# A pair of attention heads as one unit in a routed-attention and mixer kernel

## The chip, the cores and the metric

One core of a Trainium2 chip runs the whole program. Its engines work side by side and meet through semaphores: TensorE (PE, matmuls; PEld, its weight loads), VectorE (DVE), ScalarE (ACT), GpSimd (POOL) and SyncE (SP), whose queue issues most DMA transfers. The metric is the device time of one execution in microseconds (us), the median of several runs. A profile gives one execution, instruction by instruction.

## The reference

The program is routed attention followed by an MLP mixer, on 4 batches, 8 heads, 768 positions, head size 64, 16 clusters.

```python
q_assign = argmax(q_n @ c_n.T)            # nearest of 16 centroids, normalised
k_assign = argmax(k_n @ c_n.T)
mask = q_assign[:, :, :, None] == k_assign[:, :, None, :]
scores = where(mask, q @ k.T / 8, -1e9)
attn = exp(scores - max); attn = attn / (attn.sum + 1e-9)
x = (attn @ v), heads side by side         # (4, 768, 512)

h  = relu(x.T @ w_tok1) @ w_tok2           # over positions, 256 wide
u  = x + h.T
out = u + relu(u @ w_ch1) @ w_ch2          # over channels, 1536 wide
```

All inputs and outputs are float32.

## The kernel before

Two heads are taken together, so there are 16 pairs (`NPAIR`). Heads lie on partitions 0 to 63 and 64 to 127. The 768 queries are worked in two halves (`qh`) of 384; the 768 keys are six chunks (`j`) of 128.

The mask costs no vector work: one-hot cluster vectors (`ohT`, bf16, a query's multiplied by a huge negative number) are multiplied on TensorE into the same PSUM tile as q and k, so that scores of other clusters are pushed far below and their exponential is 0.

```python
def scores(g, qh):
    for j in range(NJ):                               # six chunks of keys
        sc = ps_sc.tile([P, 2, 512], F32, tag="sc")   # 3 buffers in PSUM
        for src, start in ((st["ohT"], True), (st["T"], False)):
            for h in range(2):                        # 64-row tiles of the array
                nc.tensor.matmul(sc[:, h, 0:HS], lhsT=src[rows, 1, j], rhs=src[rows, 0, js], ...)
        ex = st["ex", j] = work.tile([P, 2, HS], F32) # 6 buffers
        nc.scalar.activation(out=ex, in_=sc[:, :, 0:HS], func=ACT.Exp, scale=SM_SCALE)

def add_up(g, qh):        # VectorE: five additions of 128 x 768, for the denominators
def values(g, qh):        # TensorE: av (64-column tiles) += va^T ex, six chunks; ScalarE copies av to avT
```

Small products on TensorE belong to each pair, with VectorE work behind them:

```python
def pair_sums(g, den)         # ones^T sum: denominators, 32-column tiles
def pair_denominators(g)      # VectorE 32x32 transposes of den
def pair_reciprocals(g)       # VectorE
def route_products(g, pr)     # centroids times turned q and k, 32-column tiles
def route(g)                  # VectorE: transpose, maximum, one-hots (oh)
def route_big(g)              # VectorE: the query's one-hots times the large number
def route_turn(g)             # SP: dma_start_transpose oh -> ohT
def route_count(g)            # ScalarE: counts for a guard at the end
def half_turn(g, qh, px)      # TensorE: three 128x128 transposes of avT
def half_out(g, qh)           # VectorE: px times reciprocals -> x
def turn(g)                   # VectorE: 32x32 transposes, turned q and k (st["T"])
def load(g)                   # SP: eight loads of q and k (128-byte rows), one of v
```

The MLP weights are loaded and rounded beside attention, in 21 steps (`rounding(n)` does the next n). Step i does the last part of piece i-2, the ScalarE part of piece i-1 and issues the load of piece i:

```python
def step(i=i):
    if 2 <= i: rest(...)                     # VectorE: wh, wh, wT (one buffer); GpSimd: wT + wup -> weight
    if 1 <= i <= len(pieces): scalar_part()  # ScalarE: wh and wup from raw
    if i < len(pieces): load_bits()          # SP: raw (3 buffers) from memory, 384 or 512 KB
```

The loop:

```python
for g in range(NPAIR):
    more, old, final = g < NPAIR - 1, g - 1, g == NPAIR - 1
    if g + 2 < NPAIR: load(g + 2)
    scores(g, 0)
    if g == 0: turn(1)
    add_up(g, 0); rounding(1); values(g, 0)
    two = ps_sc.tile([P, 2, 512], F32, tag="sc", name="small")
    pair_sums(old, two[:, 0, 0:HS]);  route_products(g + 1, two[:, 1, 0:HS])
    pair_denominators(old)
    route(g + 1); route_big(g + 1); route_turn(g + 1)
    pair_reciprocals(old)
    scores(g, 1)
    route_count(g + 1)
    add_up(g, 1); turn(g + 2); values(g, 1)
    two = ps_sc.tile([P, 2, 512], F32, tag="sc", name="px")
    half_turn(old, 0, ...); half_turn(old, 1, ...); half_out(old, 0); half_out(old, 1)
    rounding(g < EARLY or final)             # EARLY = 6
# ... conditions for the first and last pairs cut
```

Ahead of the loop a start-up part loads pair 0, routes it by TensorE transposes, and keeps TensorE warm with dummy matmuls. Behind it come the mixer's matmuls (`ph`, `pu`, then blocked products `pX`, `pY`, `pZ`), which the change does not touch.

Of the kernel before, what the change touches and what calls it, by code (L numbers as in the profile page):

```python
# [17 lines left out]
C = 16  # L18
P = 128
# [11 lines left out]
QP = P // NQ  # L31
NPAIR = B * NF

EARLY = 6
SM_SCALE = 0.125


# [8 lines left out]
def kernel(  # L46
# [37 lines left out]
            tc.tile_pool(name=name, bufs=bufs, reuse_waits="tile", **kw)  # L84
        )

    ps_w = pool("ps_w", 1, space=PSUM)
    ps_av = pool("ps_av", 1, space=PSUM)
    ps_sc_stack = fast.enter_context(ExitStack())
    ps_sc = pool("ps_sc", 3, ps_sc_stack, space=PSUM)  # L90

# [4 lines left out]
    staging = fast.enter_context(ExitStack())  # L96
    stage = pool("stage", 2, staging)
    attention = fast.enter_context(ExitStack())
    loads = pool("loads", 3, attention)
    small = pool("small", 2, attention)  # L100
    qktp = pool("qktp", 2, attention)
    work = pool("work", 6, attention)
    sums = pool("sums", 2, attention)

    routing = fast.enter_context(ExitStack())
# [24 lines left out]
    def load(g):  # L130


        b, f = divmod(g, NF)
        st = state.setdefault(g, {})
        st["qk"] = qkpool.tile([P, 2, NJ, NQ, QP], F32, name="qk")
        st["va"] = loads.tile([P, 2, NJ, D], F32, name="va")
        for a, src in ((1, k), (0, q)):
            for c in range(NQ):
                h, d0 = 2 * f + c // 2, (c % 2) * QP
                nc.sync.dma_start(  # L140
                    st["qk"][c * QP : (c + 1) * QP, a].rearrange("r j i d -> r (j i) d"),
                    src[b, h, :, d0 : d0 + QP].rearrange("(i r j) d -> r j i d", i=NQ, j=NJ),
                )
        nc.sync.dma_start(
            st["va"], v[b, 2 * f : 2 * f + 2].rearrange("h (p j) d -> p h j d", p=P)
        )
# [91 lines left out]
    def centroids_norm(cen):  # L238
        sq = rsmall.tile([P, D], F32, name="censq")
        ss = rsmall.tile([P, 1], F32, name="ss")  # L240
        nc.vector.tensor_tensor(out=sq, in0=cen, in1=cen, op=ALU.mult)
        nc.vector.reduce_sum(out=ss, in_=sq, axis=AX.X)
        lo = rsmall.tile([P, 1], F32, name="lo")
        nc.vector.tensor_scalar_max(out=lo, in0=ss, scalar1=float(2.0**-100))


        nrm = rsmall.tile([P, 1], F32, name="nrm0")
        nc.vector.tensor_scalar(
            out=nrm.bitcast(I32), in0=lo.bitcast(I32), scalar1=0.5, scalar2=float(0x1FBB6875),
            op0=ALU.mult, op1=ALU.add,  # L250
        )
        for it in range(2):
            rr = rsmall.tile([P, 1], F32, name="rr")
            nc.vector.reciprocal(out=rr, in_=nrm)
            tw = rsmall.tile([P, 1], F32, name="tw")
            nc.vector.scalar_tensor_tensor(
                out=tw, in0=ss, scalar=rr, in1=nrm, op0=ALU.mult, op1=ALU.add
            )
            nrm = rsmall.tile([P, 1], F32, name="nrm")
            nc.vector.tensor_scalar(  # L260
                out=nrm, in0=tw, scalar1=(0.5, 0.49984956)[1 - it], scalar2=(0.0, 1e-6)[it],
                op0=ALU.mult, op1=ALU.add,
            )
        rden = rsmall.tile([P, 1], F32, name="rden")
        nc.vector.reciprocal(out=rden, in_=nrm)
        cn = rsmall.tile([P, 2, D], F32, name="cn")
        nc.vector.tensor_scalar_mul(
            out=cn, in0=cen.unsqueeze(1).to_broadcast([P, 2, D]), scalar1=rden
        )
        pc = ps_w.tile([P, H * C], F32, tag="w", name="pc")  # L270
        nc.tensor.transpose(out=pc, in_=cn.rearrange("p i d -> p (i d)"), identity=ident)
        return pc

# [72 lines left out]


    def load_first():
        st = state[0] = {"qk": qkpool.tile([P, 2, NJ, NQ, QP], F32, name="qk")}
        st["va"] = loads.tile([P, 2, NJ, D], F32, name="va")  # L350
        st["T"] = qktp.tile([P, 2, NJ, P], F32, name="qkT")
        st["ohT"] = qktp.tile([P, 2, NJ, P], BF16, name="ohT")
        st["rows"] = st.pop("qk").rearrange("p a j i d -> p (a j i d)").rearrange(
            "p (n a j h d) -> p n a j h d", n=2, a=2, h=2, j=HJ
        )
        for n in range(2):
            for a, src, queue in ((1, k, nc.sync), (0, q, nc.scalar)):
                for h in range(2):
                    queue.dma_start(
                        st["rows"][:, n, a, :, h],  # L360
                        src[0, h].rearrange("(p j) d -> p j d", p=P)[:, HJ * n : HJ * n + HJ],
                    )
        nc.sync.dma_start(st["va"], v[0, 0:2].rearrange("h (p j) d -> p h j d", p=P))

    def turn_first(n, tiles):

        st = state[0]
        js = slice(HJ * n, HJ * n + HJ)
        for a in (1, 0):
            for j in range(HJ):  # L370
                nc.tensor.transpose(
                    out=tiles[a][:, j * P : (j + 1) * P],
                    in_=st["rows"][:, n, a, j].rearrange("p h d -> p (h d)"), identity=ident,
                )
        return [(st["T"][:, a, js].rearrange("p j t -> p (j t)"), tiles[a]) for a in range(2)]

    def route_turn_first(n):
        po = ps_w.tile([P, 2, HJ, P], BF16, tag="w", name="po")
        for a in (1, 0):
            for j in range(HJ):  # L380
                nc.tensor.transpose(
                    out=po[:, a, j], in_=ohs[0][:, a, HJ * n + j], identity=identb
                )
        return po
# [21 lines left out]
    def scores(g, qh):  # L406
        st = state[g]
        js = slice(HJ * qh, HJ * qh + HJ)
        for j in range(NJ):
# [3 lines left out]
            for src, start in ((st["ohT"], True), (st["T"], False)):  # L413
                for h in range(2):
# [2 lines left out]
                        sc[:, h, 0:HS], lhsT=src[rows, 1, j], rhs=src[rows, 0, js],  # L417
                        start=start, stop=not start,
                    )
            ex = st["ex", j] = work.tile([P, 2, HS], F32, name="ex")  # L420
            nc.scalar.activation(out=ex, in_=sc[:, :, 0:HS], func=ACT.Exp, scale=SM_SCALE)  # L421

    def add_up(g, qh):
        st = state[g]
        if qh == 0:
            st["sum"] = sums.tile([P, 2, 2, HS], F32, name="sum")
        acc = st["sum"][:, qh]
        for j in range(1, NJ):
            nc.vector.tensor_tensor(  # L429
                out=acc, in0=acc if j > 1 else st["ex", 0], in1=st["ex", j], op=ALU.add  # L430
            )

    def values(g, qh):
        st = state[g]
        av = ps_av.tile([P, HS], F32, name="av")
        for j in range(NJ):
            ex = st.pop(("ex", j))
            for h in range(2):
                nc.tensor.matmul(  # L439
                    av[h * D : (h + 1) * D], lhsT=st["va"][:, h, j], rhs=ex[:, h],  # L440
# [285 lines left out]
            nc.vector.tensor_reduce(out=good[:, i : i + 1], in_=ok, axis=AX.X, op=ALU.min)  # L726

    def fits_count():
        pn = ps_w.tile([1, 3], F32, tag="w", name="pn")
        nc.tensor.matmul(pn, lhsT=ones[:, 0:1], rhs=good, start=True, stop=True)  # L730
        nc.vector.tensor_copy(out=count, in_=pn)

# [8 lines left out]
    def begin():  # L741
# [11 lines left out]
        for oh in ohs:  # L753
            nc.gpsimd.memset(oh, 0.0)
        load(1)
        pw = ps_av.tile([P, HS], F32, name="av")

        def keep_warm(n):
            for _ in range(n):
# [29 lines left out]
    for b in range(B):  # L789
        if b + 1 < B:  # L790
            ends += [lambda b=b, t=t: tok1(b + 1, t) for t in range(NT)]
        ends += [lambda b=b, j=j: tok2(b, j) for j in range(NJ)]

    def rounding(n):
        for _ in range(min(n, len(weights))):
            weights.pop(0)()

    for g in range(NPAIR):
        more, old, final = g < NPAIR - 1, g - 1, g == NPAIR - 1
        if g + 2 < NPAIR:  # L800
            load(g + 2)
        if final:
            assert not weights
            routing.close()
            W["ch2"] = pool("wc2pool", 1, side="right").tile([P, NCT, DM], F32, name="wc2")
            weights = list(weight_steps(stage, W, ("ch2",)))

        scores(g, 0)
        if g == 0:
            turn(1)  # L810
        add_up(g, 0)
        rounding(1)
        values(g, 0)
        if more or old >= 0:
            two = ps_sc.tile([P, 2, 512], F32, tag="sc", name="small")
            if old >= 0:
                pair_sums(old, two[:, 0, 0:HS])
            if more:
                route_products(g + 1, two[:, 1, 0:HS])
            if old >= 0:  # L820
                pair_denominators(old)
            if more:
                route(g + 1)
                route_big(g + 1)
                route_turn(g + 1)
            if old >= 0:
                pair_reciprocals(old)

        scores(g, 1)
        if more:  # L830
            route_count(g + 1)
        add_up(g, 1)
        if g + 2 < NPAIR:
            turn(g + 2)
        values(g, 1)
        if old >= 0:
            two = ps_sc.tile([P, 2, 512], F32, tag="sc", name="px")
            for qh in range(2):
                half_turn(old, qh, two[:, qh, 0:HS])
            for qh in range(2):  # L840
                half_out(old, qh)
        rounding(g < EARLY or final)

    pair_sums(NPAIR - 1, ps_w.tile([P, HS], F32, tag="w", name="den"))
    pair_denominators(NPAIR - 1)
    pair_reciprocals(NPAIR - 1)
    ps_sc_stack.close()
    pools["ps_m"] = pool("ps_m", 2, space=PSUM)
    for m in range(9):
        ends.pop(0)()  # L850
        if m == 0:
            half_turn(NPAIR - 1, 0, ps_w.tile([P, HS], F32, tag="w", name="px"))
            half_turn(NPAIR - 1, 1, ps_av.tile([P, HS], F32, name="av"))
            for qh in range(2):
                half_out(NPAIR - 1, qh)
        if m % 3 == 2:
# [243 lines left out]
```

## Time and profile before

| | |
|---|---|
| time, median of 3 runs | 877.95 us (877.77 to 878.12) |
| span of the profiled execution | 875.5 us |
| start of the first scores | 10.14 us |
| start of the first mixer matmul (`ph`) | 333.06 us |
| one exponential, 128x768, on ScalarE | 811 ns |
| one addition, 128x768, on VectorE | 958 ns median |
| turning q and k of a pair, VectorE | 2 x 953 ns |

An engine's line in the busy table is the time in which it had an instruction running, its share of the span, and the number of instructions. In the slices each digit is a fortieth of the span, in tenths busy. The chain of waits is read back from the last instruction; each of its rows is a start, a length, an engine, a name and line, and how many instructions were merged. In a timeline a row reads: start, length, engine, line, operation, output<-inputs, shapes, count, and in brackets the idle time before it with what ended it. A matmul's row length holds its way through the array, so neighbouring matmuls overlap, and their cost is read from the distance between starts. A DMA row's last number is the median from issue to landing.

### The profile page before, as it was taken

How to read it: one execution, taken by the hardware profiler on the slowest of the kernel's cores; microseconds unless marked ns; L12 is line 12 of the kernel's file. 1: busy time of each engine (PE TensorE's matmuls, PEld its weight loads, DVE VectorE, ACT ScalarE, POOL GpSimd, SP SyncE). 2: the span in 40 equal slices, each digit the busy share in tenths (PEclk: the TensorE clock that was granted, in tenths of full speed). 3: DMA queues.
4: the chain of work that ended last, by engine and by line, in shares of the span. 5: the costliest groups of instructions: out<-in, count | busy, mean ns of one | idle time of the engine just before them, and what ended most of it. 6: DMA issues, size and time to landing. Idle time of an engine off the chain costs nothing.

```text
span 875.5 us, 11022 instructions
## 1 busy us (share of the span) xinstructions
PE 862.4 (99%) x4294; PEld 522.8 (60%) x4294; DVE 504.9 (58%) x848; ACT 297.8 (34%) x506; POOL 44.2 (5%) x40
## 2 busy tenths in 40 slices
PE   9999999999999999999999999999999999999996
PEld 4444444444444444444578686685876867768675
DVE  6798898888878862895553433423344333443332
ACT  4666566666556551321210211203112031130210
POOL 1010011000010000330000000000000000000000
PEclk9999999999999999999999999999999999999999
DMA  8665675544443130420000010000010000100001
GB/s 153 156 123 119 140 139 115 126 109 97 97 97 73 20 90 0 144 72 1 0 1 1 0 37 37 0 1 0 36 38 1 0 1 25 48 1 1 0 25 51
DMA packets 133275, 47.61 MB, mean 54 GB/s; under 512 B 122080, under 2 KB 126176, under 8 KB 133216
## 3 DMA queue, kind: packets, MB, share of 16 engines
q1 hardware_dynamic: 131616, 46.45, 23.0%
q8 instruction: 35, 0.57, 0.3%
q10 hardware_dynamic: 1600, 0.39, 0.2%
q14 instruction: 24, 0.20, 0.1%
HBM read 34.64 MB, written 6.29 MB: 47 GB/s over the span
## 4 chain that ended last, share of the span: by engine, by line
PE 95%; DVE 3%; ACT 1%; issue 0%; DVEq 0%
PE sc L416 18%; PE av L439 15%; PE pX L690 14%; PE pX L639 14%; PE pZ L690 7%; PE pZ L639 7%; PE ph L508 4%; PE pY L690 4%; PE pY L639 4%; PE pu L517 3%; PE px L468 1%; PE small L455 1%; PE pt L580 1%; PE small L296 1%; DVE wh L209 1%; DVE wT L214 1%
## 5 line engine op out<-in xcount | busy, mean ns | idle before, releaser
L421 ACT ACTIVATE ex<-sc 128x768 f32<-128x768 f32 x192 | 152.6, 811 | 44.8 <-PE sc L416 42.6
L416 PE MATMUL sc<-qkT 64*128 64x384 f32 x768 | 155.1, 482 | 0.0
L429 DVE TENSOR_TENSOR sum<-sum,ex 128x768 f32<-128x768 f32 x128 | 125.3, 979 | 13.7 <-ACT ex L421 0.5
L439 PE MATMUL av<-ex,va 128*64 128x384 f32 x768 | 130.9, 490 | 0.0
L439 PEld LDWEIGHTS av<-ex,va 128*64 128x64 f32 x768 | 52.2, 137 | 74.8 <-issue 71.0
L416 PEld LDWEIGHTS sc<-qkT 64*128 64x128 f32 x768 | 68.2, 188 | 34.8 <-issue 34.6
L639 PE MATMUL pX<-uT,wc 128*128 128x384 f32 x192 | 67.4, 487 | 0.0
L416 PE MATMUL sc<-ohT 64*128 64x384 bf16 x384 | 63.0, 324 | 0.3 <-DVE ohT L389 0.2
L647 ACT COPY p<-pX 128x384 f32<-128x384 f32 x24 | 11.4, 475 | 148.1 <-PE pX L639 148.1
L639 PEld LDWEIGHTS pX<-uT,wc 128*128 128x128 f32 x192 | 36.2, 190 | 24.7 <-issue 1.0
L221 POOL TENSOR_TENSOR wc<-wT,wup 128x512 int32<-128x512 int32 x24 | 32.0, 1334 | 253.5 <-ACT avT L446 132.0
L429 DVE TENSOR_TENSOR sum<-ex 128x768 f32<-128x768 f32 x32 | 32.0, 1001 | 20.3 <-ACT ex L421 20.2
L446 ACT COPY avT<-av 128x384 f32<-128x384 f32 x32 | 15.3, 479 | 83.1 <-PE av L439 83.1
L508 PE MATMUL ph<-x,wt 128*128 128x512 f32 x96 | 42.0, 594 | 1.2 <-DVE x L520 0.7
L517 PE MATMUL pu<-h,wt 128*128 128x512 f32 x96 | 42.0, 592 | 0.0
L534 DVE TENSOR_TENSOR c<-pZ,u 128x384 f32<-128x384 f32 x24 | 13.4, 557 | 46.9 <-PE pZ L639 46.9
L416 PEld LDWEIGHTS <-ohT 64*128 64x128 bf16 x384 | 19.2, 94 | 35.4 <-issue 13.6
L534 DVE TENSOR_TENSOR x<-pX,x 128x256 f32<-128x256 f32 x24 | 10.2, 423 | 49.3 <-PE pX L690 49.3
L534 DVE TENSOR_TENSOR hA<-pY,p 128x384 f32<-128x384 f32 x24 | 13.4, 557 | 40.4 <-PE pY L639 40.4
L690 PE MATMUL pX<-w2s,hA 128*128 128x256 f32 x144 | 35.1, 380 | 0.5 <-DVE x L534 0.5
L690 PE MATMUL pX<-wc,hA 128*128 128x256 f32 x144 | 35.0, 379 | 0.0
L690 PE MATMUL pZ<-w2s,hS 128*128 128x256 f32 x144 | 35.0, 379 | 0.0
(129 smaller groups left out, 1196.5 us busy)
## 6 DMA issues: line engine op xcount, KB each, us to landing
raw<-in_moe_w_ch_dram SPq DMA_DIRECT2D x24, 512.0 KB, 4.3
qk<-in_k_dram SPq DMA_DIRECT2D x64, 96.0 KB, 4.0
va<-in_v_dram SPq DMA_DIRECT2D x16, 384.0 KB, 4.0
out_dram<-x SPq DMA_DIRECT2D x24, 256.0 KB, 2.0
qk<-in_q_dram SPq DMA_DIRECT2D x60, 96.0 KB, 3.4
raw<-in_moe_w_tok_dram SPq DMA_DIRECT2D x3, 512.0 KB, 4.6
raw<-in_moe_w_tok_dram SPq DMA_DIRECT2D x4, 384.0 KB, 4.0
qk<-in_q_dram ACTq DMA_DIRECT2D x4, 96.0 KB, 3.1
```

Of the source, the lines that this page charges most:

```text
L221: nc.gpsimd.tensor_tensor(out=dst.bitcast(I32), in0=T, in1=up, op=ALU.add)
L416: nc.tensor.matmul(sc[:, h, 0:HS], lhsT=src[rows, 1, j], rhs=src[rows, 0, js], start=start, stop=not start,)
L421: nc.scalar.activation(out=ex, in_=sc[:, :, 0:HS], func=ACT.Exp, scale=SM_SCALE)
L429: nc.vector.tensor_tensor(out=acc, in0=acc if j > 1 else st["ex", 0], in1=st["ex", j], op=ALU.add)
L439: nc.tensor.matmul(av[h * D : (h + 1) * D], lhsT=st["va"][:, h, j], rhs=ex[:, h], start=(j == 0), stop=(j == NJ - 1),)
L446: nc.scalar.copy(out=st["avT"][:, js].rearrange("p j t -> p (j t)"), in_=av)
L508: nc.tensor.matmul(pf, lhsT=W["tok1"][:, j, t * P : (t + 1) * P], rhs=xs[b][:, j], start=(j == 0), stop=(j == NJ - 1),)
L517: nc.tensor.matmul(pu, lhsT=W["tok2"][:, t, j], rhs=h1s[b][:, t], start=(t == 0), stop=(t == NT - 1))
L534: nc.vector.tensor_tensor(out=dst, in0=a, in1=b, op=ALU.add)
L639: nc.tensor.matmul(psum, lhsT=A[a][:, k, c * P : (c + 1) * P], rhs=R[r][:, k], start=start and k == 0, stop=k == 1, skip_group_check=not s ...
L647: nc.scalar.copy(out=kept[name], in_=psum)
L690: nc.tensor.matmul(psum, lhsT=h2[a][:, k, i * P : (i + 1) * P], rhs=Bw[w][:, 3 * part + k], start=start and k == 0, stop=k == 2, skip_grou ...
```

## The change

A pair becomes one unit. All twelve chunks of scores (both query halves) run in one go, then all twelve of values, and then the pair's small products at one place: the transposes of the pair before, the sums of this pair, and the routing products of the pair after next. It is meant to let TensorE change between kinds of products less often. For that the exponentials get nine buffers instead of six (three more chunks can stand in PSUM), `av` gets two PSUM buffers (it takes over the bank of `ps_w`), v is loaded apart from q and k with two buffers instead of three, and routing runs two pairs ahead instead of one. The weight steps, of which there are still 21, are done at one place: two in even pairs below 12, else one.

```diff
-EARLY = 6
+EARLY = 12
+EX = 9
...
-    ps_w = pool("ps_w", 1, space=PSUM)
-    ps_av = pool("ps_av", 1, space=PSUM)
+    ps_av = pool("ps_av", 2, space=PSUM)
...
-    loads = pool("loads", 3, attention)
+    loads = pool("loads", 2, attention)
...
-    work = pool("work", 6, attention)
+    work = pool("work", EX, attention)
...
+    def route_on(g):
+        route(g)
+        route_big(g)
+        route_turn(g)
...
+    load_v(1)
     for g in range(NPAIR):
-        [the loop above]
+        final = g == NPAIR - 1
...
+        for qh in range(2):
+            scores(g, qh)
+            if g == 0 and qh == 0:
+                turn(1)
+                load(2)
+            add_up(g, qh)
         if g == 0:
+            route_products(1, ps_av.tile([P, HS], F32, tag="av", name="pr"))
+            route_on(1)
+        for other in (1, 2) if g == 1 else (g + 1,) if 2 <= g < NPAIR - 1 else ():
+            route_count(other)
         if g + 2 < NPAIR:
             turn(g + 2)
+        if g + 3 < NPAIR:
+            load(g + 3)
+        rounding(2 if final or g % 2 == 0 and g < EARLY else 1)
+        for qh in range(2):
+            values(g, qh)
+        if g + 2 < NPAIR:
+            load_v(g + 2)
+
+        if g > 0:
             two = ps_sc.tile([P, 2, 512], F32, tag="sc", name="px")
             for qh in range(2):
+                half_turn(g - 1, qh, two[:, qh, 0:HS])
+        two = ps_sc.tile([P, 2, 512], F32, tag="sc", name="small")
+        pair_sums(g, two[:, 0, 0:HS])
+        if g + 2 < NPAIR:
+            route_products(g + 2, two[:, 1, 0:HS])
+        if g > 0:
             for qh in range(2):
+                half_out(g - 1, qh)
+        pair_denominators(g)
+        if g + 2 < NPAIR:
+            route_on(g + 2)
+        pair_reciprocals(g)
```

Cut: in the start-up part the first rows of q and k are held in two of the nine exponential buffers instead of a q-and-k buffer, and the products that used `ps_w` use a buffer of `av`.

More of the change, by code (lines that the diff above doesn't have):

```diff
@@ L135, in load @@
         st["qk"] = qkpool.tile([P, 2, NJ, NQ, QP], F32, name="qk")
-        st["va"] = loads.tile([P, 2, NJ, D], F32, name="va")
         for a, src in ((1, k), (0, q)):
@@ L143, in load, with load_v @@
                 )
+    def load_v(g):
+        b, f = divmod(g, NF)
+        st = state[g]
+        st["va"] = loads.tile([P, 2, NJ, D], F32, name="va")
         nc.sync.dma_start(
@@ L269, in centroids_norm @@
         )
-        pc = ps_w.tile([P, H * C], F32, tag="w", name="pc")
+        pc = ps_av.tile([P, H * C], F32, tag="av", name="pc")
         nc.tensor.transpose(out=pc, in_=cn.rearrange("p i d -> p (i d)"), identity=ident)
@@ L348, in load_first @@
     def load_first():
-        st = state[0] = {"qk": qkpool.tile([P, 2, NJ, NQ, QP], F32, name="qk")}
-        st["va"] = loads.tile([P, 2, NJ, D], F32, name="va")
+        st = state[0] = {}
         st["T"] = qktp.tile([P, 2, NJ, P], F32, name="qkT")
         st["ohT"] = qktp.tile([P, 2, NJ, P], BF16, name="ohT")
-        st["rows"] = st.pop("qk").rearrange("p a j i d -> p (a j i d)").rearrange(
-            "p (n a j h d) -> p n a j h d", n=2, a=2, h=2, j=HJ
-        )
+        st["rows"] = [
+            work.tile([P, 2, HS], F32, name="ex").rearrange("p a (j h d) -> p a j h d", h=2, d=D)
+            for _ in range(2)
+        ]
         for n in range(2):
@@ L359, in load_first @@
                     queue.dma_start(
-                        st["rows"][:, n, a, :, h],
+                        st["rows"][n][:, a, :, h],
                         src[0, h].rearrange("(p j) d -> p j d", p=P)[:, HJ * n : HJ * n + HJ],
                     )
-        nc.sync.dma_start(st["va"], v[0, 0:2].rearrange("h (p j) d -> p h j d", p=P))
     def turn_first(n, tiles):
@@ L372, in turn_first @@
                     out=tiles[a][:, j * P : (j + 1) * P],
-                    in_=st["rows"][:, n, a, j].rearrange("p h d -> p (h d)"), identity=ident,
+                    in_=st["rows"][n][:, a, j].rearrange("p h d -> p (h d)"), identity=ident,
                 )
@@ L377, in route_turn_first @@
     def route_turn_first(n):
-        po = ps_w.tile([P, 2, HJ, P], BF16, tag="w", name="po")
+        po = ps_av.tile([P, 2, HJ, P], BF16, tag="av", name="po")
         for a in (1, 0):
@@ L419, in scores @@
                     )
-            ex = st["ex", j] = work.tile([P, 2, HS], F32, name="ex")
+            ex = st["ex", qh, j] = work.tile([P, 2, HS], F32, name="ex")
             nc.scalar.activation(out=ex, in_=sc[:, :, 0:HS], func=ACT.Exp, scale=SM_SCALE)
@@ L425, in add_up @@
         if qh == 0:
-            st["sum"] = sums.tile([P, 2, 2, HS], F32, name="sum")
+            st["sum"] = sums.tile([P, 2, 2, HS], F32, name="sum", bufs=1)
         acc = st["sum"][:, qh]
@@ L429, in add_up @@
             nc.vector.tensor_tensor(
-                out=acc, in0=acc if j > 1 else st["ex", 0], in1=st["ex", j], op=ALU.add
+                out=acc, in0=acc if j > 1 else st["ex", qh, 0], in1=st["ex", qh, j], op=ALU.add
             )
@@ L434, in values @@
         st = state[g]
-        av = ps_av.tile([P, HS], F32, name="av")
+        av = ps_av.tile([P, HS], F32, tag="av", name="av")
         for j in range(NJ):
-            ex = st.pop(("ex", j))
+            ex = st.pop(("ex", qh, j))
             for h in range(2):
@@ L728, in fits_count @@
     def fits_count():
-        pn = ps_w.tile([1, 3], F32, tag="w", name="pn")
+        pn = ps_av.tile([1, 3], F32, tag="av", name="pn")
         nc.tensor.matmul(pn, lhsT=ones[:, 0:1], rhs=good, start=True, stop=True)
@@ L755, in begin @@
         load(1)
-        pw = ps_av.tile([P, HS], F32, name="av")
+        load_v(0)
+        pw = ps_av.tile([P, HS], F32, tag="av", name="av")
         def keep_warm(n):
@@ L796, in rounding @@
             weights.pop(0)()
+    load_v(1)
     for g in range(NPAIR):
-        more, old, final = g < NPAIR - 1, g - 1, g == NPAIR - 1
-        if g + 2 < NPAIR:
-            load(g + 2)
+        final = g == NPAIR - 1
         if final:
@@ L806 @@
             weights = list(weight_steps(stage, W, ("ch2",)))
-        scores(g, 0)
-        if g == 0:
[L810 to L832, printed above, removed]
+        for qh in range(2):
[4 more added lines that the diff above has]
+            add_up(g, qh)
+        if g == 0:
+            route_products(1, ps_av.tile([P, HS], F32, tag="av", name="pr"))
+            route_on(1)
+        for other in (1, 2) if g == 1 else (g + 1,) if 2 <= g < NPAIR - 1 else ():
+            route_count(other)
@@ L833 @@
         if g + 2 < NPAIR:
             turn(g + 2)
-        values(g, 1)
-        if old >= 0:
+        if g + 3 < NPAIR:
[6 more added lines that the diff above has]
+        if g > 0:
             two = ps_sc.tile([P, 2, 512], F32, tag="sc", name="px")
             for qh in range(2):
-                half_turn(old, qh, two[:, qh, 0:HS])
-            for qh in range(2):
-                half_out(old, qh)
@@ L842 @@
[L842 to L846, printed above, removed]
+                half_turn(g - 1, qh, two[:, qh, 0:HS])
[4 more added lines that the diff above has]
+        if g > 0:
+            for qh in range(2):
+                half_out(g - 1, qh)
@@ L851 @@
         if m == 0:
-            half_turn(NPAIR - 1, 0, ps_w.tile([P, HS], F32, tag="w", name="px"))
-            half_turn(NPAIR - 1, 1, ps_av.tile([P, HS], F32, name="av"))
+            half_turn(NPAIR - 1, 0, ps_av.tile([P, HS], F32, tag="av", name="px"))
+            half_turn(NPAIR - 1, 1, ps_av.tile([P, HS], F32, tag="av", name="av"))
             for qh in range(2):
```

## The prediction

> **What bounds the kernel now.** I read the busy table first, then the slices, then the chain that ended last, then the timelines of single engines and of the DMA queue.
>
> ```profile
> PE 862.4 (99%) x4294; PEld 522.8 (60%) x4294; DVE 504.9 (58%) x848; ACT 297.8 (34%) x506; POOL 44.2 (5%) x40
> PE   9999999999999999999999999999999999999996
> ```
>
> TensorE (PE) is busy in every slice, so only two things count: what shortens its own stream, and what makes it wait. The attention loop is the first 333 us (the first `ph` matmul starts at 333.06). One steady pair of heads in the chain of waits (start us, us):
>
> ```profile
> 231.60 4.95 PE sc L416 x36
> 236.55 4.02 PE av L439 x24
> 240.57 0.78 PE small L455 x8
> 241.35 0.65 PE small L296 x8
> 242.00 4.95 PE sc L416 x36
> 246.95 4.02 PE av L439 x24
> 250.97 0.81 PE px L468 x6
> ```
>
> The next pair would begin at 251.78: 20.18 us, and TensorE waits for nobody in it. Now the pieces. Within a run of scores the timeline of TensorE shows one chunk every 0.8075 us:
>
> ```profile
> 232.35 0.33 PE L416 MATMUL sc<-ohT 64*128 64x384 bf16 x2
> ...
> 235.58 0.33 PE L416 MATMUL sc<-ohT 64*128 64x384 bf16 x2
> ```
>
> (235.58 - 232.35) / 4 = 0.8075. Six chunks are 4.845, the row has 4.95: 0.105 is lost at the turn from scores to values. The weight loads of values come every 0.322 us for two matmuls (from 227.07 to 229.97 in nine steps), so 24 matmuls are 3.87 and the row has 4.02: 0.15 is lost at the turn from values to the next kind.
>
> The other view that matters is the DMA queue, SP, in the first pairs, with the landing times of the page (last number, us):
>
> ```profile
> 22.78 1.58 SPq L341 DMA_TRANSPOSE ohT<-oh  x1
> 24.41 0.84 SPq L191 DMA_DIRECT2D raw<-in_moe_w_tok_dram  x1
> 25.30 3.45 SPq L140 DMA_DIRECT2D qk<-in_k_dram  x4
> 28.79 3.42 SPq L140 DMA_DIRECT2D qk<-in_q_dram  x4
> ```
>
> ```profile
> raw<-in_moe_w_tok_dram SPq DMA_DIRECT2D x3, 512.0 KB, 4.6
> ohT<-oh SPq DMA_TRANSPOSE x15, 3.8
> ```
>
> SP issues in program order. It sat from 20.6 until 22.78 for VectorE's one-hots, and all transfers behind the transposing one started after it. The eight loads of q and k take 5.8 to 6.9 us just to issue.
>
> **What the Trainium skill says.** *TensorEngine Tiling (Array Packing)*, Key Properties: changing the tiling mode drains TensorE. The trace agrees in kind: scores are 64*128 tiles, values 128*64, sums and routing 128*32, transposes 128*128, and each turn costs 0.1 to 0.15 us. *TensorE: Matmul & The Clock Gate*, Part 1, "Architectural detail": the queues of ScalarE and VectorE are strictly first in, first out; nothing in the trace overtakes. Same page, "What's actually happening": after an idle window of about 3.4 us TensorE falls to half clock and needs about as long of full work to come back. The trace has the cold start: twelve warm-up matmuls of 384 columns take 4.02 us, 0.335 each, where a bf16 matmul of 384 columns later costs 0.16 (0.8075 less 0.645 of float32 passes). The clock column shows 1.00 all the same, so I go by the durations. *Trainium Kernel Development and Optimization*, Key Constraints: the queues share 16 DMA engines, so it is the sequencer's issue order that I look at.
>
> **The change, part by part.**
>
> *Removed: turns.* Before, a pair has six: scores-values twice, values-small, small-scores, values-px, px-scores. After: scores-values, values-px, px-small, small-scores. A pair is 12 x 0.8075 + 0.105 = 9.795, 48 x 0.161 + 0.15 = 7.89, px 0.81 (the same 0.81 lies before a 128*32 product at 330.97 to 331.78), small 0.78 + 0.65 = 1.43. Sum 19.92, against 20.18: 0.26 less. For 16 pairs -4.1 us. The number of chunks, exponentials and additions does not change.
>
> *Added: exponentials 9 to 11 wait.* Nine buffers for twelve chunks: nine are written out, three scores stand in PSUM until values has read the first buffers. ScalarE starts 1.03 after the scores (242.96 against 241.93) and needs 0.807 each; number 9 can start when values has done one chunk, at 9.795 + 0.65 + 0.4 (tail of the last matmul) = 10.85. Number 11 ends at 13.3, and values wants it at 9.8 + 11 x 0.645 = 16.9. No wait. VectorE adds until 14.8 (1.03 each), turns the next q and k (1.83) until 16.6, rounds one weight piece (0.42 + 0.43 + 0.69, with gaps 1.6) until 18.2; px is ready at 18.6. No wait either.
>
> *Moved: two rounding steps at one place.* In even pairs below 12, VectorE rounds two pieces in a row, and `wT` has one buffer, read by GpSimd for 1.27 to 1.33 us. The second piece ends at about 20.3. The two `half_out` (1.02) and the two 32x32 transposes (0.58, 0.54) come after it, and chunks 1 and 2 of the next pair want their PSUM buffers at 20.7 and 21.5; they come free at about 21.4 and 22.4. That is some 0.9 us in pairs 2, 6, 8, 10 (in pair 4 the pieces are smaller, in pair 0 nothing is rounded yet): +3.5.
>
> *Moved: the first pair.* Here I expect the largest term. Routing of pair 1 now stands after all of pair 0's additions. Scores start at 10.14 as before; twelve chunks with `po` between them end at 20.4, the routing product at 21.2, values follow. Exponential 9 starts at 22.1, 11 ends at 24.5, the additions end at 26.0, the routing on VectorE takes 2.15 (20.57 to 22.72 before): 28.15. The transposing DMA lands 3.8 later, 32.0. TensorE, done with values at 29.1 and with both small products at 30.9 (it waits for the turned q and k until 30.0), starts pair 1 at about 32.0: 1 us lost.
>
> Worse is what SP holds behind that transfer. The build's order on SP is: transpose (waits for VectorE), eight loads for pair 3, then the first two weight pieces. So the first `raw` is issued at 28.2 + 1.5 + 6.0 = 35.7 and lands at 40.3. On ScalarE its `wh` and `wup` stand ahead of both `avT` copies and of all exponentials of pair 1: 40.3 + 1.3 + 0.9 = 42.4, first exponential until 43.2. Scores has three PSUM buffers and stops after three chunks, at 34.5. It stands still 8.8 us. An idle TensorE of that length should come back cold: half of about 4 us lost, +2. In later pairs the piece lands at 14 to 15 us after the scores' start, before the place where ScalarE wants it, so it happens once.
>
> Sum: -4.1 (turns) + 3.5 (double rounding) + 1.0 (late one-hots) + 8.8 (stall) + 2.0 (clock) = +11.2, so 889; I write 888, as the 3.5 is more likely too large than too small. The dense stage after the loop has the same instructions and no change.
>
> **The rivals.**
>
> 1. *Only the turns count: 874 (-4.1).* For it: TensorE is the bound in the whole trace, and buffers are counted to fit (nine and three make twelve). Against it: the first pair's queue order, which no buffer mends. This holds only if the first raw piece lands before about 33 us, and I see no way for it to.
> 2. *The stall but no double-rounding loss and no cold clock: 884.* VectorE has 58% of the span, though about 85% in the loop; a half microsecond of slack in the even pairs would do. This is near my lower end.
> 3. *Exponentials or additions become the bound in every pair: 893 or more.* VectorE's work in a pair is about 17 to 18.5 us of 19.92. If the additions run slower while GpSimd rounds (one addition took 1841 ns against a median of 958), each pair could lose 0.3 us, +5.
> 4. *A faster loop than the turns explain.* Nothing supports more: every product remains.
>
> **Range and chances.** Loss at the start between 8 and 14, double rounding 0 to 4, turns -3 to -5: 880.5 to 895. Over 2% faster would need 860.4, and the loop has no such idle time: 0.01. Over 2% slower is 895.5: 0.06. The rest 0.93.
>
> **What would show it.** In the changed profile: pairs without double rounding 19.9 us apart; an idle stretch on TensorE from about 34.5 to 43 us with ScalarE's `wh` waiting for the raw piece; matmuls of double length for some 4 us after it; the transposing DMA issued near 28 us and raw near 36; 0.5 to 1 us waits at the start of pairs 3, 7, 9, 11. Wrong would be: no idle stretch there (then 874 to 878), a steady pair of more than 20.2 us (then a new wait that I have not seen), or scores waiting for exponentials in the middle of a run.

## The result and the profile after

| | before | changed |
|---|---|---|
| time, median | 877.93 us (877.77 to 878.12) | 889.97 us (888.85 to 890.51) |
| ratio | | 1.0135, 95% interval 1.0118 to 1.0153 |
| first scores | 10.14 us | 10.49 us |
| first mixer matmul (`ph`) | 333.06 us | 345.39 us |

The kernel became 1.35% slower. The whole difference arises ahead of the first `ph`: 12.3 us.

The busy table and two rows of slices of the changed kernel:

```profile
PE 862.1 (97%) x4294; PEld 525.7 (59%) x4294; DVE 502.2 (57%) x848; ACT 295.8 (33%) x506; POOL 42.4 (5%) x40
PE   9599999999999999999999999999999999999996
PEclk9889999999999999999999999999999999999999
```

TensorE has one hole, in the second slice (22 to 44 us). The third row, the TensorE clock that was granted in tenths of full speed, drops in that slice and in the next one; before, it was 9 throughout. Everywhere else TensorE is as busy as before.

A steady pair in the chain of waits of the changed kernel (start us, us):

```profile
104.89 9.80 PE sc L420 x72
114.69 7.89 PE av L443 x48
122.58 0.81 PE px L472 x6
123.39 0.78 PE small L459 x8
124.17 0.65 PE small L301 x8
```

The next pair starts at 124.81: 19.92 us against 20.18 before. The turns were worth what they were meant to be.

Where time was lost shows in the timelines of the first two pairs. The DMA queue, SP:

```profile
14.97 4.09 SPq L140 DMA_DIRECT2D qk<-in_q_dram  x4
28.80 1.55 SPq L346 DMA_TRANSPOSE ohT<-oh  x1
30.40 3.04 SPq L140 DMA_DIRECT2D qk<-in_k_dram  x4
33.48 3.52 SPq L140 DMA_DIRECT2D qk<-in_q_dram  x4
37.05 1.12 SPq L196 DMA_DIRECT2D raw<-in_moe_w_tok_dram  x2
```

It issues nothing from 19.1 to 28.80, until VectorE has the one-hots of pair 1, then eight loads for pair 3, and only at 37.05 the weight pieces. ScalarE (in brackets the idle time and what ended it):

```profile
22.53 2.21 ACT L425 ACTIVATE ex<-sc 128x768 f32<-128x768 f32 x3 [3.19 <-PE av L443]
41.40 0.66 ACT L202 ACTIVATE wh<-raw 128x512 f32<-128x512 f32 x1 [16.66 <-DMA raw<-in_moe_w_tok_dram]
41.96 0.65 ACT L204 ACTIVATE wup<-raw 128x512 int32<-128x512 uint32 x1
42.50 0.85 ACT L450 COPY avT<-av 128x384 f32<-128x384 f32 x2
43.23 2.23 ACT L425 ACTIVATE ex<-sc 128x768 f32<-128x768 f32 x3
```

It waits 16.66 us for that piece while three chunks of scores stand in PSUM. TensorE:

```profile
34.39 0.33 PE L420 MATMUL sc<-ohT 64*128 64x384 bf16 x2
34.55 0.81 PE L420 MATMUL sc<-qkT 64*128 64x384 f32 x4
44.12 0.50 PE L420 MATMUL sc<-ohT 64*128 64x384 bf16 x2 [8.76 <-ACT ex L425]
44.39 1.51 PE L420 MATMUL sc<-qkT 64*128 64x384 f32 x4
45.67 0.55 PE L420 MATMUL sc<-ohT 64*128 64x384 bf16 x2
...
48.87 0.47 PE L420 MATMUL sc<-ohT 64*128 64x384 bf16 x2
...
49.82 0.34 PE L420 MATMUL sc<-ohT 64*128 64x384 bf16 x2
```

After 8.76 idle us chunks come every 1.55 us (45.67 - 44.12) or a little more until 48.87, then every 0.8 again. A table by stretches shows the granted clock beside it. A row has start and end, length, the busy time of PE, PEld, DVE, ACT and POOL (with their instructions), then the granted clock, the DMA share and GB/s:

```profile
44.00:48.00 4.00, 3.88 (x16) 2.35 (x17) 2.87 (x3) 2.68 (x5) 0.00 (x0) 0.50 1.13 168
```

The granted clock was 0.50 there.

Last, the turn from pair 2 to pair 3, VectorE, GpSimd and TensorE in one timeline:

```profile
80.81 0.43 DVE L214 TENSOR_SCALAR wh<-wh 128x512 uint32<-128x512 uint32 x1
81.34 0.69 DVE L219 SCALAR_TENSOR_TENSOR wT<-raw,wh 128x512 uint32<-128x512 uint32 x1
82.18 1.32 POOL L226 TENSOR_TENSOR wt<-wT,wup 128x512 int32<-128x512 int32 x1 [18.71 <-DVE wT L219]
82.41 1.38 DVE L214 TENSOR_SCALAR wh<-wh 128x512 uint32<-128x512 uint32 x1
83.88 0.69 DVE L219 SCALAR_TENSOR_TENSOR wT<-raw,wh 128x512 uint32<-128x512 uint32 x1
84.49 1.02 DVE L480 TENSOR_TENSOR x<-px,rcps 128x384 f32<-128x384 f32 x2
85.56 0.34 PE L420 MATMUL sc<-ohT 64*128 64x384 bf16 x2 [0.57 <-DVE x L480]
```

The second rounding ends at 84.57, then come the outputs that free px, and scores waits. From one routing product to the next the pairs are 19.92 us apart, but 20.82 from pair 2 to 3, and the same after 6, 8 and 10; 20.03 after 4.

### The profile page after: what moved, and what is told of

It reads as the page before. It is cut to its first block, busy times and chain, and to the rows that moved or that the text cites. A ratio compares the mean times of both kernels' runs of the same rounds, so it can differ in the third digit from the quotient of the medians.

```text
span 887.9 us, 11037 instructions
## 1 busy us (share of the span) xinstructions
PE 862.1 (97%) x4294; PEld 525.7 (59%) x4294; DVE 502.2 (57%) x848; ACT 295.8 (33%) x506; POOL 42.4 (5%) x40
## 4 chain that ended last, share of the span: by engine, by line
PE 84%; DVE 8%; SPq 3%; DMA 2%; ACT 1%; issue 1%; DVEq 0%; ACTq 0%
PE sc L420 14%; PE pX L694 14%; PE pX L643 14%; PE av L443 10%; PE pZ L694 7%; PE pZ L643 7%; PE ph L512 4%; PE pY L694 4%; PE pY L643 3%; PE pu L521 3%; SPq L140 3%; DVE wh L214 2%; DVE wT L219 1%; PE pt L584 1%; PE px L472 1%; DVE wh L209 1%
## 5 line engine op out<-in xcount | busy, mean ns | idle before, releaser
L420 PE MATMUL sc<-qkT 64*128 64x384 f32 x768 | 157.2, 488 | 0.0
L433 DVE TENSOR_TENSOR sum<-sum,ex 128x768 f32<-128x768 f32 x128 | 122.7, 958 | 37.4 <-ACT ex L425 25.6
L443 PE MATMUL av<-ex,va 128*64 128x384 f32 x768 | 127.6, 488 | 1.3 <-DVE sim L317 1.3
L202 ACT ACTIVATE wh<-raw 128x512 f32<-128x512 f32 (+1 forms) x31 | 20.7, 668 | 53.5 <-DVE wT L219 27.4
L433 DVE TENSOR_TENSOR sum<-ex 128x768 f32<-128x768 f32 x32 | 29.8, 931 | 11.9 <-ACT ex L425 11.9
```

The source lines that it names most:

```text
L202: nc.scalar.activation(out=p["h"].bitcast(F32), in_=p["hi"].bitcast(F32), func=ACT.Abs)
L433: nc.vector.tensor_tensor(out=acc, in0=acc if j > 1 else st["ex", qh, 0], in1=st["ex", qh, j], op=ALU.add)
L443: nc.tensor.matmul(av[h * D : (h + 1) * D], lhsT=st["va"][:, h, j], rhs=ex[:, h], start=(j == 0), stop=(j == NJ - 1),)
```

## The experiments

Theory: the raw piece held on SP stops ScalarE and TensorE once, TensorE comes back cold, and the double rounding costs 0.9 us four times. Rivals: the late one-hots of pair 1 are the cause; the long matmuls have another reason; VectorE's total work counts and not where it stands. All runs are compared with the kernel before, whose medians beside them were 877.7 to 877.9.

**The raw piece, moved half the way.**

```diff
+        rounding(2 if final or g % 2 == 0 and g < EARLY else 1)
         if g + 3 < NPAIR:
             load(g + 3)
-        rounding(2 if final or g % 2 == 0 and g < EARLY else 1)
```

> The weight pieces are issued ahead of the eight loads of q and k, still behind the transposing DMA. Theory (the first raw piece, held on the SP queue, stops ScalarE and then TensorE in pair 1): raw is issued at about 30.4 instead of 37.05 and lands at 34.7; scores of pair 1 stand still for some 2.3 us instead of 8.9, too short for TensorE to come back cold: -6.6 and -2.5, so about 881. Rival (the late one-hots of pair 1, or the transposing DMA itself, are what costs): 890, unchanged.

Measured: 881.52 us, ratio 1.0041 (1.0026 to 1.0055). Its SP and TensorE:

```profile
29.54 1.55 SPq L346 DMA_TRANSPOSE ohT<-oh  x1
31.14 1.37 SPq L196 DMA_DIRECT2D raw<-in_moe_w_tok_dram  x2
```
```profile
38.30 0.34 PE L420 MATMUL sc<-ohT 64*128 64x384 bf16 x2 [2.27 <-ACT ex L425]
38.46 0.82 PE L420 MATMUL sc<-qkT 64*128 64x384 f32 x4
39.10 0.34 PE L420 MATMUL sc<-ohT 64*128 64x384 bf16 x2
```

The transfer goes out 5.9 us earlier and the standstill falls to 2.27. The chunks behind it have their full pace. One-hots are as late as before (pair 1 starts its scores at 33.43, in an execution whose first scores were 0.74 later too), so the rival falls.

**The raw piece, ahead of the transposing DMA.**

```diff
             if g == 0 and qh == 0:
                 turn(1)
                 load(2)
+                rounding(1)
...
-        rounding(2 if final or g % 2 == 0 and g < EARLY else 1)
+        rounding(2 if final or g % 2 == 0 and 0 < g < EARLY else 1)
```

> The first weight load is issued right after the loads for pair 2, ahead of the transposing DMA that waits for VectorE. Theory: no standstill in pair 1 and no cold matmuls, -8.9 and -2.5: about 878.6, and the double roundings still cost 0.9 each in pairs 2, 6, 8, 10. Rival (late one-hots): 890.

Measured: 878.39 us, ratio 1.0007 (0.9998 to 1.0015). Raw is issued at 18.96, and pair 1 has no standstill. 11.6 us of the changed kernel's time hung on the place of one line.

**TensorE kept warm, first attempt.** Dummy matmuls write the unused columns of the third chunk's scores tile, emitted after its exponential.

```diff
+            if (g, qh, j) == (1, 0, 3):
+                for _ in range(150):
+                    nc.tensor.matmul(sc[:, 0, HS:512], lhsT=warm[:, 0:P], rhs=warm[:, P : 2 * P], start=True, stop=True)
             sc = ps_sc.tile([P, 2, 512], F32, tag="sc", name="sc")
```

> The changed kernel with 150 dummy bf16 matmuls of 128 columns on TensorE in the standstill of pair 1, into unused columns of a scores tile; nothing else moves. Theory (TensorE comes back at half clock after 8.9 idle us): the chunks after the standstill take 0.81 us at once, -2.5: about 887.5. Rival (the doubled matmuls come from something else at that time, such as the transfers): 890.

Measured: 900.37 us; the dummies missed the standstill. They share a tile with the exponential that reads it, so they waited for it:

```profile
46.43 10.91 PE L419 MATMUL sc<-warm 128*128 128x128 bf16 x150 [10.43 <-ACT ex L431]
57.27 0.34 PE L426 MATMUL sc<-ohT 64*128 64x384 bf16 x2
```

They came after the standstill and added to it.

**TensorE kept warm, mended.** The same dummies ahead of the third exponential (`(1, 0, 2)`, before `ex` is allocated).

> Mends the run with the dummy matmuls: the 150 dummies now stand ahead of the third exponential in the program, so that they run during the standstill of pair 1 and not after it. Theory (half clock after 8.9 idle us): the chunks after the standstill take 0.81 us at once, -2.5 against the changed kernel: about 887.5. Rival (the doubled matmuls come from something else at that time): 890.

Measured: 887.57 us, ratio 1.0110 (1.0093 to 1.0126), 2.40 below the changed kernel.

```profile
35.28 8.55 PE L427 MATMUL sc<-warm 128*128 128x128 bf16 x150
44.01 0.34 PE L420 MATMUL sc<-ohT 64*128 64x384 bf16 x2 [0.18 <-ACT ex L431]
44.17 0.82 PE L420 MATMUL sc<-qkT 64*128 64x384 f32 x4
44.82 0.34 PE L420 MATMUL sc<-ohT 64*128 64x384 bf16 x2
```

Scores go on at the same moment, now at 0.81 us a chunk at once. And the same 150 dummies took 10.91 us after an idle stretch and 8.55 without one. The granted clock stays at 1.00 from 28 to 52 us in this run. The half clock is shown, with its price.

**The single `wT` buffer taken away.** On the run with the early raw piece; `T` is written over `wh`, which gets three buffers.

```diff
-            bufs = 1 if name == "wT" else 2
+            bufs = 3 if name == "wh" else 2
...
-            T = tmp("wT", U32, p["n"])
+            T = h
```

> As the run with the early raw piece, and the rounded piece is put together in place in wh (three buffers), so that the single wT buffer is gone. My prediction's mechanism (the second piece waits until GpSimd has read wT): the even pairs lose less, by 0.5 to 0.9 us in each of four pairs, so 875 to 876.6. Rival (the second L214 instruction lasts 1.38 instead of 0.43 us because GpSimd runs at the same time, whatever the buffer): no change against that run, about 878.6.

Measured: 877.23 us, ratio 0.9994 (0.9987 to 1.0001): 1.16 less, where 2 to 3.6 was expected of my mechanism. The pairs after the double roundings are 20.68 apart instead of 20.81: the buffer was worth 0.13 each. About half of the 1.16 doesn't lie in the loop at all: from the first `ph` to the end this run takes 541.7 us, the run with the early raw piece 542.3. L214 still takes 1.38 us in the second piece (71.49), and most of the loss stays, so most of it isn't the buffer.

**A control, and the rounding in another order.** Control: `wup` is written in place too, into the low words of raw.

```diff
-            p["up"] = tmp("wup", I32, p["n"])
+            p["up"] = p["lo"].bitcast(I32)
```

> Control for the next run: as the run without the wT buffer, and wup is written in place into the low words of raw, so that neither wT nor wup exists; the order of the rounding is unchanged. Both theories: the second L214 still lasts 1.38 us in the even pairs, pairs 3, 7, 9, 11 still lose 0.8 us each, about 877.2.

Measured: 877.39 us, ratio 0.9998 (0.9989 to 1.0007), pairs after double roundings 20.70 apart, L214 again up to 1.40 us. Then, on it, both pieces' first two VectorE steps come ahead of both last ones (`h_part` is L209 and L214 of the changed kernel, `T_part` is L219 and GpSimd's addition):

```diff
-    rest(piece i-2);  scalar_part(i-1);  load_bits(i);  rest(piece i-1);  scalar_part(i);  load_bits(i+1)
+    scalar_part(i-1);  h_part(i-2);  h_part(i-1);  T_part(i-2);  load_bits(i);  T_part(i-1);  scalar_part(i);  load_bits(i+1)
```

> As the control, but where two pieces are rounded in a row VectorE does L209 and L214 of both pieces first and then the two L219; GpSimd's first addition can only start after the first L219, beside the second L219 or later. Theory (VectorE and GpSimd exclude each other on a shared SBUF port, and the one that starts first holds it): no VectorE instruction is stretched, because the second L219 starts before GpSimd does; GpSimd waits instead; the pairs after the even ones start on time, -0.8 x 4: about 874.0. Rival (GpSimd slows whatever VectorE does beside it, by a share of bandwidth): the second L219 takes the 1.0 us instead of L214, no change against the control, 877.2.

Measured: 874.27 us, ratio 0.9962 (0.9948 to 0.9976). VectorE and GpSimd at such a place:

```profile
189.22 0.42 DVE L213 TENSOR_SCALAR wh<-wh 128x512 f32<-128x512 f32 x1
189.67 0.43 DVE L218 TENSOR_SCALAR wh<-wh 128x512 uint32<-128x512 uint32 x1
190.02 1.28 DVE L225 SCALAR_TENSOR_TENSOR wh<-raw,wh 128x512 uint32<-128x512 uint32 x2
```
```profile
190.83 2.87 POOL L232 TENSOR_TENSOR wc<-wh,raw 128x512 int32<-128x512 int32 x2 [19.30 <-DVE wh L225]
```

No VectorE instruction is stretched, not even the second L225 (L219 of the changed kernel), during which GpSimd starts. GpSimd's two additions take 2.87 us instead of twice 1.29; all of the excess is in the first, which takes 1.62. So now GpSimd is the one that waits. From pair 2 on all pairs are 19.92 apart. The same instructions in another order are 3.1 us faster.

**The second rounding at the end of the pair.** Back on the run with the early raw piece.

```diff
-        rounding(2 if final or g % 2 == 0 and 0 < g < EARLY else 1)
+        rounding(2 if final else 1)
...
         pair_reciprocals(g)
+        rounding(g % 2 == 0 and 0 < g < EARLY)
```

> As the run with the early raw piece, and in the even pairs the second rounding step stands at the end of the pair, after the reciprocals, instead of beside the first. Theory (two roundings in a row make VectorE late for the px and small buffers): the 0.8 to 0.9 us at the start of pairs 3, 7, 9, 11 and 0.1 at pair 5 go, -3.6: about 874.7. Rival (VectorE's total work in those pairs is the cause, wherever it stands): additions and one-hots come later instead, 877 to 878.4.

Measured: 874.76 us, ratio 0.9962 (0.9948 to 0.9976), all pairs from 2 on 19.92 apart. VectorE has the same work in them, so its total is not the cause.

**The first pair.** On top of that, `route_products(1, ...)` and `route_on(1)` move into the loop over halves, after `add_up(0, 0)`.

> As the run with the split rounding, and pair 1 is routed between the two halves of pair 0's scores, as in the kernel before. Theory: the 1.3 us wait for the av buffer and the 0.3 us for the one-hots of pair 1 go, two turns of 0.1 come in once: about 873.2. Rival (the first pair is bound by the start-up transfers): 874.7, unchanged.

Measured: 872.92 us (872.78 to 873.39), ratio 0.9944 (0.9928 to 0.9961): faster than both kernels. The chain of waits in its first pairs:

```profile
21.45 7.89 PE av L443 x48
29.34 0.78 PE small L459 x8
30.12 0.65 PE small L301 x8
30.77 9.80 PE sc L420 x72
40.56 7.89 PE av L443 x48
```

No wait is left in the loop. The first `ph` starts at 328.21, 4.85 earlier than in the kernel before.

**The halves interleaved again.** On that version, `values(g, 0)` moves up behind `add_up(g, 0)`.

> As the run with the first pair routed earlier, but with scores, values, scores, values in each pair as in the kernel before; the small products stay at one place. Two more turns of TensorE in each of 16 pairs. Theory (a turn costs 0.105 from scores to values and 0.15 from values to the next kind): +0.255 x 16 = +4.1, about 877.3. Rival (the turns cost nothing by themselves, and the pair is shorter for its fewer waits): no change, 873.2.

Measured: 881.00 us, ratio 1.0033 (1.0020 to 1.0046): +8.1 instead of +4.1. In the chain:

```profile
117.69 4.02 PE av L443 x24
121.71 4.95 PE sc L420 x36
```

Six chunks take 4.95 and twelve 9.80; half the values take 4.02 and all of them 7.89: 0.10 and 0.15 for the two turns, as reckoned, 4.1 in 16 pairs. With them alone the pairs would be 20.17 apart; they are 20.2 to 20.6 apart. The other half is a new wait that I had not expected: the second half's exponentials now come later, VectorE's additions with them, and it reaches px late. In pair 7, px's outputs (L480) start at 173.73, though px was done at 172.4, and the next pair's chunk 1 starts 1.04 after its chunk 0 (174.80 - 173.76) instead of 0.81. This was read in one pair and not tested by a further run. So this run shows the price of a turn by its rows, not by its total.

## Why the prediction was right

It said 888 and a range of 880.5 to 895; measured 889.97. Term by term:

| term | predicted | measured |
|---|---|---|
| turns, per pair | 20.18 to 19.92 | 19.92; 0.10 and 0.15 per turn |
| waits ahead of pair 1 | 1.0 | 1.30 + 0.24 |
| start of pair 1 | 32.0 | 32.76 |
| raw issued, first exponential done | 35.7, 43.2 | 37.05, 44.0 |
| standstill of scores | 8.8 | 8.76 |
| half clock | 2.0 | 2.47 from the rows, 2.40 by the warm run |
| double rounding | 3.5 | 0.90 x 4 + 0.11 = 3.7 |

The half clock from the rows: nine chunks and the turn from 44.12 to 53.96 are 9.84, at full pace 9 x 0.8075 + 0.105 = 7.37.

*Turns:* right, in size too. *The stall:* right, mechanism and place; two runs that moved one transfer by 5.9 and 18 us took away 8.5 and 11.6 us. *The half clock:* right, and a little longer than 4 us: 44.12 to 48.87. The prediction went by durations because the clock column stayed at 1.00 over the cold start; in the standstill the column did show it, 0.50. *Exponentials 9 to 11:* no wait, as said.

*Double rounding:* the size was right and the mechanism wrong. I said that the second piece waits because GpSimd still reads the single `wT`. Without that buffer only 0.13 of the 0.9 went. What holds it is the instruction L214 itself, 1.38 us instead of 0.43, whenever GpSimd's addition is already running: in the changed kernel's loop that is every second piece of a double rounding (1.38 or 1.39 at 82.4, 163.1, 203.8, 244.6; 1.07 for the smaller piece at 122.8) and no other. That the size fitted is partly luck: a wait for `wT` and a stretched L214 both end with the same GpSimd addition (82.18 + 1.32 = 83.50), so VectorE came out about as late as reckoned.

The Trainium skill describes it, *SBUF — State Buffer*, "SBUF: two separate sides": VectorE and GpSimd share a port pair as an exclusive lock, taken by a VectorE instruction in a two-port mode, or by one with two inputs in SBUF against a GpSimd instruction that reads SBUF; the one that starts first holds it for the whole instruction while the other blocks. The traces agree in both directions, L214 behind a GpSimd addition (1.38) and, in the reordered run, a GpSimd addition behind L225 (1.62 instead of 1.28). Which mode L214 runs in no trace here shows.

The kernel before had the sign already, in a place where TensorE did not wait for it:

```profile
52.65 0.96 DVE L429 TENSOR_TENSOR sum<-ex 128x768 f32<-128x768 f32 x1
52.77 1.96 POOL L221 TENSOR_TENSOR wt<-wT,wup 128x512 int32<-128x512 int32 x1 [11.78 <-DVE wT L214]
53.72 3.96 DVE L429 TENSOR_TENSOR sum<-sum,ex 128x768 f32<-128x768 f32 x3
```

GpSimd started just behind an addition of VectorE and took 1.96 us instead of 1.27; then the next addition of VectorE took 1.84 instead of 0.96. The prediction names such an addition, of 1841 ns, in its third rival, and fears that GpSimd slows the additions; that the rounding's own VectorE instructions can be held the same way it does not consider.

*Missed:* a wait of 1.30 us in the first pair. The routing product of pair 1 takes one of the two `av` buffers, and values of the second half waits until VectorE, behind ten additions, has read it (27.00, waiting for L317). It did not set the start of pair 1: after it TensorE still waited 0.24 us for the one-hots to land (32.76), so the predicted cause, late one-hots, decided that start. Part of the 0.76 by which it was later than reckoned is a start of the scores 0.35 later, which isn't due to the change: with the same start-up code the other runs had their first scores at 10.15 to 11.23. Routing pair 1 earlier took both waits away and gave 1.84 us.

*Sums:* the three terms of the range add up to 880.9 and 892.9, so the stated 880.5 to 895 has some room at both ends, more at the upper one; 48 x 0.161 + 0.15 is 7.88, not 7.89, and 40.3 + 1.3 + 0.9 is 42.5, not 42.4. Nothing hangs on these.

*Rival 1 (only the turns count):* its mechanism was right and its sum, 874, is what the kernel gives once the late transfer and the stretched rounding are out: 874.27 and 874.76. Routing pair 1 earlier gives 872.92.

## What to carry to other kernels

Lengthening a unit of work moves everything that hung in its middle: a DMA queue in program order, with one transfer in it that waits for an engine, hands that wait to every transfer behind it, and from there to engines that have nothing to do with it. When an order is changed, follow each queue's first items through the start-up, where no lead has been built up yet; a steady state that is 0.26 us better per pair was worth 4 us, and one late transfer cost 11. And before counting buffers, ask whether two engines can run those instructions side by side at all; an instruction that takes twice its usual time in the trace before is a reason to ask.

## What the runs showed of the hardware

- TensorE after 8.76 us of idleness ran at half pace for 4.75 us (granted clock 0.50) and lost 2.4; after 2.27 idle us (the run with raw moved half the way) it did not slow down. 150 dummy matmuls of 128 columns, 8.55 us, kept it at full pace.
- One VectorE instruction of 0.43 us took 1.38 when GpSimd had started an addition of 1.3 us just before it; with the order of starts turned round, GpSimd took the delay (1.62 instead of 1.28). It does not show as idle time of either engine, only as a longer instruction.
- In the three runs with the reordered rounding, the second rounding at the end of the pair, and pair 1 routed earlier, the pairs from 2 on are 19.91 to 19.93 us apart.
